# Two quarters of an up-projection weight moved from casting transfers on GpSimd's queue to plain transfers on SyncE's queue, with the cast done by three engines

## The chip, the core and the metric

The kernel runs on one core of one Trainium2 chip. A core has a matrix engine (TensorE; PE in the profile), three engines for elementwise work (VectorE, DVE; ScalarE, ACT; GpSimd, POOL), a queue engine (SyncE, SP) and 16 DMA engines that all queues share. Transfers can be issued by SP, ACT and POOL. In this kernel only those issued by POOL change the type on the way. The metric is the device time of one execution in microseconds (us): the kernel before took 323.79 us as the median of three runs (322.96 to 326.55).

## The reference

Sliding-window attention with a linear bias, followed by a two-layer feed-forward block with a hardswish between the layers. Eight batches, eight heads, 576 positions, head size 64, window 128; 4608 tokens, model size 512, inner size 2048. Everything is float32 outside the kernel.

```python
scores = (1/sqrt(64)) * q @ k.T            # per batch and head
scores = where((0 <= i-j) & (i-j < 128), scores + slope[h] * -(|i-j|), -1e9)
attn   = softmax(scores)
x      = (attn @ v)  -> [4608, 512]        # heads side by side
h      = x @ w_in                          # [512, 2048]
g      = h * clip(h + 3, 0, 6) / 6
out    = g @ w_out                         # [2048, 512]
```

## The kernel before

All matrix products are in bf16. The whole instruction order of each engine is written out by hand, so every engine works through its own list in that order and waits in place. A batch is four groups `g` of two heads; groups 0 to 3 are batch 0, groups 4 to 7 batch 1.

**Attention of one group.** k and q come as float32, are cast to bf16 (`prepare` for batch 0, `prepare_double` for batches 1 and 2), and are transposed on TensorE (`transposes`, `wide_double`, `double`) with a copy out of PSUM by DVE or ACT. `scores_diag` and `scores_off` compute the scores of the diagonal and of the preceding block, ACT takes the exponentials (`exp_diag`, `exp_off_full`), `attend` multiplies by v and DVE normalises. `back` transposes the result on TensorE into the one PSUM buffer `ps_o`, and ACT copies it into `xT`; for group 3 ACT copies 256 columns and DVE the rest. The next `back` cannot start before the last copy has emptied that buffer.

**Feed-forward.** Tokens are taken 512 at a time. `moe_up(nt, ms)` multiplies four slices `ks` of `w_in_sb`, 128 columns `ms` at a time, with the four group rows of `xT` (slice `ks` needs group `ks`), then ACT takes a ReLU (L470) and DVE the min and product into `gbuf[nt % 2]` (L471). `moe_down` multiplies by `w_out_sb` and DVE stores. `fill(n)` emits the next n such steps between the attention steps. `up_begin(nt, ms, n)` does the first n slices of a `moe_up` ahead.

**Weights.** `w_in_sb` is [128, 4, 2048] in bf16. It is loaded in four quarters of 512 columns by `load_w_in(g)` (L166): one transfer issued by POOL that reads 1 MB of float32 and writes 512 KB of bf16. Columns `ms` 0 to 3 are quarter 0, 4 to 7 quarter 1. Quarter 0 is issued by POOL among its casts of v of batch 0. Quarter 1 follows a one-column memset of `w_out_sb` (`second_w_in`, L176), which holds POOL until groups 0 and 1 have been attended. Quarters 2 and 3 come among the casts of k and q of batch 1.

**Loads.** SP issues, in this order: q of batch 0 (4 transfers; ACT issues the four of k), v of batch 0 (5, in 256-byte pieces), k and q of batch 1 (`load_double`, L98: k, k, q, q for the first two groups, then the same for the other two), v of batch 1 (5), k and q of batch 2. Each transfer issued by SP or ACT takes one of eight semaphores in turn, and so waits until the transfer eight places before it has landed.

**Buffers.** `gbuf[0]` and `gbuf[1]` are [128, 16, 512] bf16 each. `gbuf[0]` is first written by the L471 of `moe_up(0, 0)`, its upper half by `moe_up(0, 8)` and later. `gbuf[1]` holds the exponentials of batch 1 (its upper half those of groups 6 and 7), and `w_out_sb` those of batch 0.

The end of `first_batch` and the few steps after it carry the change. The engines' lists there, in words:

- ACT: eight exponential passes of batch 0; the four copies of `back`; the ReLU of `moe_up(0, 0)`; a copy of transposed k (L256); two more ReLUs; the exponentials of group 4, and so on.
- POOL: the casts of v; the issue of quarter 0; the memset and the issue of quarter 1; the casts of k, q of batch 1, groups 4 and 5 (four), then of groups 6 and 7 (k, k, issue of quarter 2, q, q, issue of quarter 3).
- TensorE: `attend` and `back` of groups 0 to 3, `up_begin(0, 0, 3)` ahead of `back(3)`, the transposes of q (`wide_double`), `up_begin(0, 1, 3)`, the rest of `moe_up(0, 0)`, the transposes of k, `moe_up(0, 1)` and `(0, 2)`, the transposes of k of groups 6 and 7, the scores of group 4.

Of the kernel before, what the change touches and what calls it, by code (L numbers as in the profile page):

```python
# [10 lines left out]
FP32 = mybir.dt.float32  # L11
# [7 lines left out]
def kernel(  # L19
# [9 lines left out]
    nc = tc.nc  # L29
# [13 lines left out]
    n_ms = d_ff // 128  # L43
    n_ks = d_model // 128
# [9 lines left out]
    w_in_sb = perm.tile([128, n_ks, d_ff], BF16)  # L54
    w_out_sb = perm.tile([128, n_ms, d_model], BF16)
# [22 lines left out]
    gbuf = [held.tile([128, n_ms, NT], BF16, name=f"gbuf{i}") for i in range(2)]  # L78
# [17 lines left out]
    def load_double(b, dp, nm, eng):  # L96
        for e in range(2):
            eng.dma_start(out=ldbuf["qk".index(nm)][:, ds((2 * dp + e) * RT * D, RT * D)],  # L98
                          in_=src_of[nm][b, ds(4 * dp, 4), :, :].rearrange(
                              "(i e) (a t) d -> e a i (t d)", e=2, t=RT)[e])  # L100
# [7 lines left out]
    def load_tokens(b, nm):  # L108
        t = tokens(b, nm)
        for j in range(NQ):  # L110
            n = min(128, S - j * 128)
            nc.sync.dma_start(out=t[:n, j, :, :],
                              in_=src_of[nm][b, :, ds(j * 128, n), :].rearrange("h p d -> p h d"))

    def constants():
        make_identity(nc, ident)
        nc.vector.memset(bias3, 0.5)
        nc.vector.memset(warm, 0.0)
        nc.scalar.activation(out=warm, in_=warm, func=ACT.Exp)
        nc.gpsimd.iota(rel_i, pattern=[[0, 1]], base=0, channel_multiplier=1)  # L120
        base = rpool.tile([128, NT], FP32, tag="r6", name="base")
        base_i = base[:, 0:256].bitcast(INT32).rearrange("p (s c) -> p s c", s=2)
        base_b = base[:, 256:384].bitcast(BF16).rearrange("p (s c) -> p s c", s=2)
        nc.gpsimd.iota(base_i, pattern=[[128, 2], [0, 128]], base=-192, channel_multiplier=1)
        nc.gpsimd.tensor_copy(out=base_b, in_=base_i)
        biases()
        nc.gpsimd.affine_select(out=base_b[:, 1, :], in_=base_b[:, 1, :], pattern=[[1, 128]],
                                channel_multiplier=-1, base=0,
                                compare_op=ALU.is_ge, fill=-(2.0 ** 30))
        nc.gpsimd.affine_select(out=base_b[:, 0, :], in_=base_b[:, 0, :], pattern=[[-1, 128]],  # L130
                                channel_multiplier=1, base=-1,
                                compare_op=ALU.is_ge, fill=-(2.0 ** 30))
        nc.vector.memset(kTb[0][:, :, 4, LAST:128], 0.0)
        for h in range(H):
            nc.vector.tensor_scalar(out=tab[:, h, :, :], in0=base_b, scalar1=slopes[h] / scale,
                                    scalar2=0.0, op0=ALU.mult, op1=ALU.add)
# [28 lines left out]
    def load_w_in(g):  # L165
        nc.gpsimd.dma_start(  # L166
            out=w_in_sb[:, :, ts(g, 512)],
            in_=moe_w_in[:, ts(g, 512)].rearrange("(k p) f -> p k f", p=128))

    def load_w_out(g):  # L170
        nc.gpsimd.dma_start(
            out=w_out_sb[:, ts(g, 4), :],
            in_=moe_w_out[ds(g * 512, 512), :].rearrange("(m p) d -> p m d", p=128))

    def second_w_in():
        nc.gpsimd.memset(w_out_sb[:, 4, 0:1], 0.0)  # L176
        load_w_in(1)

    def cast_v(b, j, copy):
        n = min(128, S - j * 128)  # L180
# [42 lines left out]
    def prepare_double(b, dp, copies, nms="kq", early=None):  # L223
        for nm, copy in zip(nms, copies):
            pr = prs.tile([128, RT, 2 * D], BF16, tag=f"pr{nm}", name="pr2")
            for e in range(2):
                copy(out=pr[:, :, ts(e, D)],  # L227
                     in_=ldbuf["qk".index(nm)][:, ds((2 * dp + e) * RT * D, RT * D)].rearrange(
                         "p (t d) -> p t d", t=RT))
                if early and (nm, e) == (nms[0], 0):  # L230
                    early()
            st[b, dp, nm] = pr
# [15 lines left out]
    def wide_double(b, dp, nm, copy):  # L248
        src = st[b, dp, nm]
        wide = ps_sc.tile([128, 2, 512], FP32, tag="sc", name="tp3")  # L250
        tp = wide.rearrange("p s c -> p (s c)").bitcast(BF16)[:, 0:RT * 128].rearrange(
            "p (t c) -> p t c", t=RT)
        for t in range(RT):
            nc.tensor.transpose(tp[:, t, :], src[:, t, :], ident)  # L254
        dst = (qTb if nm == "q" else kTb)[b % 2][:, 2 * dp:2 * dp + 2, :, :]
        copy(out=dst.rearrange("p i j c -> p i (j c)")[:, :, 0:S].rearrange(  # L256
                 "p i (a t) -> p i a t", t=RT),
             in_=tp.rearrange("p t (a i) -> p i a t", i=2))
# [147 lines left out]
    def attend(g):  # L406
        wide = ps_sc.tile([128, 2, 512], FP32, tag="sc", name="wide")
        av = wide[:, :, 0:NQ * W].rearrange("p e (j c) -> p e j c", j=NQ)
        av_matmuls(g, range(NQ), lambda qt, e: av[:, e, qt, :])
        avs = st[g, "avs"] = small.tile([128, NQ, 2, D], BF16, tag="avs", name="avs")  # L410
        rc = small.tile([128, 2, NQ, 1], FP32, tag="rcw", name="rcw")
        nc.vector.reciprocal(rc, av[:, :, :, D:W])
        nc.vector.tensor_tensor(out=avs.rearrange("p j e d -> p e j d"), in0=av[:, :, :, 0:D],
                                in1=rc.to_broadcast([128, 2, NQ, D]), op=ALU.mult)
# [40 lines left out]
    def up_begin(nt, ms, n):  # L455
        hps = ps_h.tile([128, NT], FP32, tag="h", name="hps")
        up_mms(nt, ms, 0, n, hps)
        begun[nt, ms] = hps, n
# [64 lines left out]
    def fill(n):  # L523
        for _ in range(n):
            if at[0] == len(units):
                return
            nt, fn, step = units[at[0]]
            if fn is moe_up and done[0] < NP * (min((nt * NT + NT - 1) // S, B - 1) + 1):
                return
            fn(nt if fn is moe_up else nt - 1, step)  # L530
            at[0] += 1
# [26 lines left out]
    def first_batch():  # L558
        prepare(0, (V, A))
        warm_up(20)  # L560
        tables_diag(0)
        tables_off(0)
        warm_up(10)
        transposes(0, (V, A))
        scores_diag(0)
        prepare(1, (P, V))
        transposes(1, (V, V))
        scores_off(0)
        exp_full(0)
        scores_diag(1)  # L570
        prepare(2, (P, P))
        tables_off(1)
        transposes(2, (V, V))
        scores_off(1)
        exp_full(1)
        scores_diag(2)
        prepare(3, (P, V))
        tables_off(2)
        transposes(3, (V, V))
        scores_off(2)  # L580
        exp_full(2)
        scores_diag(3)
        scores_off(3)
        exp_full(3)
        cast_v(0, 0, V)
        cast_v(0, 1, P)
        load_w_in(0)
        cast_v(0, 2, V)
        cast_v(0, 3, V)
        cast_v(0, 4, P)  # L590
        for dp in range(2):
            for nm in "kq":
                load_double(1, dp, nm, nc.sync)
        load_tokens(1, "v")
        attend(0)
        attend(1)
        back(0)
        attend(2)
        back(1)
        second_w_in()  # L600
        prepare_double(1, 0, (P, P))
        attend(3)
        back(2)
        up_begin(0, 0, 3)
        back(3)
        wide_double(1, 0, "q", V)
        prepare_double(1, 1, (P,), "k")
        load_w_in(2)
        prepare_double(1, 1, (P,), "q")
        load_w_in(3)  # L610
        for dp in range(2):
            for nm in "kq":
                load_double(2, dp, nm, nc.sync)
        up_begin(0, 1, 3)
        done[0] = NP
        fill(1)
        wide_double(1, 0, "k", A)
        fill(2)

    def second_batch():  # L620
# [97 lines left out]
    with tc.manual_schedule(engines=every):  # L718
        load_run(0, "k", nc.scalar)
        load_run(0, "q", nc.sync)  # L720
        load_run(1, "k", nc.scalar)
        load_run(1, "q", nc.sync)
        for g in (2, 3):
            load_run(g, "k", nc.scalar)
            load_run(g, "q", nc.sync)
        load_tokens(0, "v")
        constants()
        memsets()
        memsets_later()
        first_batch()  # L730
        second_batch()
        fill(2)
        segment(2 * NP, G, lambda g: FILLS.get(g, (1, 1, 1, 2, 0, 1, 2)))
        done[0] = G
        fill(len(units))
# [30 lines left out]
```

## Time and profile before

| | |
|---|---|
| median of three runs | 323.79 us (322.96 to 326.55) |
| the profiled execution's own time | 323.38 us |
| its span, first to last instruction | 321.7 us |
| TensorE busy | 308.1 us (96%) |
| ACT busy | 195.1 us (61%) |
| DVE busy | 172.7 us (54%) |
| POOL busy | 140.7 us (44%) |
| granted TensorE clock | 1.000 |
| the four transfers of w_in, issue to landing | median 9.2 us (6.5 to 10.4) |

Start times in the profile count from the first instruction of the span. The profiled execution's own time is 1.68 us above its span. A busy TensorE is not necessarily at its full rate, since the ends of its pipelined products are modelled. Lines are those of the kernel before; in the changed kernel the helpers from `cast_v` (L179) to `segment` have line numbers six or more higher, because of the lines added.

### The profile page before, as it was taken

What the parts mean: (1) busy time and instruction counts of PE and PEld (TensorE: products, weight loads), DVE (VectorE), ACT (ScalarE), POOL (GpSimd) and SP (SyncE); (2) the same over time, 40 slices, a digit from 0 to 9 for tenths busy, and PEclk for the clock granted to TensorE, in tenths of its full rate; (3) what the DMA queues carried; (4) which work ended last, traced back from release to release, by engine and by line L of the source; (5) the groups of instructions that cost most, each with busy time, mean ns of one, the idle gap of its engine ahead of it and who ended that gap; (6) DMA issues with size and microseconds to landing.
All of it is one profiled execution on the core that took longest, in us unless ns stands there. A gap on an engine that the chain in (4) does not pass through costs nothing.

```text
span 321.7 us, 7010 instructions
## 1 busy us (share of the span) xinstructions
PE 308.1 (96%) x2699; PEld 166.7 (52%) x2738; DVE 172.7 (54%) x338; ACT 195.1 (61%) x334; POOL 140.7 (44%) x249
## 2 busy tenths in 40 slices
PE   6879999999999999999999999999999999999996
PEld 5465465555555455455677644554554444444443
DVE  6657675554356555555555556555655455455510
ACT  4748976877777766666676657666764344244401
POOL 8456592683494767356745664563331000000000
PEclk9999999999999999999999999999999999999999
DMA  7999999899999999999999999932112200000112
GB/s 277 202 319 225 272 255 208 223 235 204 220 223 184 220 198 201 200 223 205 186 191 191 229 176 201 211 108 86 23 53 64 76 34 35 33 33 33 67 52 79
DMA packets 131425, 51.90 MB, mean 161 GB/s; under 512 B 118976, under 2 KB 123328, under 8 KB 131392
## 3 DMA queue, kind: packets, MB, share of 16 engines
q1 hardware_dynamic: 126160, 45.36, 67.0%
q0 software_dynamic: 4224, 4.19, 8.3%
q10 hardware_dynamic: 1008, 1.90, 1.6%
q8 instruction: 21, 0.34, 0.5%
q14 instruction: 12, 0.10, 0.1%
HBM read 36.70 MB, written 9.44 MB: 143 GB/s over the span
## 4 chain that ended last, share of the span: by engine, by line
PE 82%; DMA 5%; ACT 4%; POOL 4%; issue 2%; DVE 2%; SPq 1%; POOLq 0%
PE ops L501 35%; PE hps L451 35%; DMA ldbuf<-in_q_dram 3%; PE scd L296 2%; DMA qTb<-tbuf 2%; PE av L391 2%; PE av L383 2%; ACT r L470 2%; PE sco L328 1%; PE ops L482 1%; ACT kTb L244 1%; PE tp L254 1%; POOL tbuf L194 1%; ACT gbuf L351 1%; SPq L98 1%
## 5 line engine op out<-in xcount | busy, mean ns | idle before, releaser
L471 DVE SCALAR_TENSOR_TENSOR gbuf<-r,hps 128x512 bf16<-128x512 f32 x144 | 98.7, 687 | 102.5 <-ACT r L470 100.2
L470 ACT ACTIVATE r<-hps,bias 128x512 f32<-128x512 f32 x144 | 98.9, 689 | 89.5 <-PE hps L451 88.2
L451 PE MATMUL hps<-xT,w_in_sb 128*128 128x512 bf16 (+1 forms) x621 | 142.7, 358 | 2.3 <-DMA w_in_sb<-in_moe_w_in_dram 0.9
L501 PE MATMUL ops<-w_out_sb,gbuf 128*128 128x512 bf16 x540 | 134.2, 380 | 2.3 <-issue 1.7
L451 PEld LDWEIGHTS <-w_in_sb 128*128 128x128 bf16 x640 | 58.8, 98 | 54.8 <-DMA w_in_sb<-in_moe_w_in_dram 1.3
L501 PEld LDWEIGHTS <-gbuf 128*128 128x128 bf16 x560 | 52.2, 98 | 57.2
L354 POOL TENSOR_SCALAR_AFFINE_SELECT pd<-pd 128x512 bf16<-128x512 bf16 x48 | 29.6, 631 | 34.5 <-ACT pd L351 34.4
L364 POOL TENSOR_SCALAR_AFFINE_SELECT po<-po 128x512 bf16<-128x512 bf16 x48 | 30.1, 633 | 32.7 <-ACT po L361 32.6
L351 ACT ACTIVATE pd<-scd,bias_d 128x512 bf16<-128x512 f32 x48 | 31.6, 685 | 5.0 <-PE scd L296 3.6
L194 POOL CAST tbuf<-ldbuf 128x512 bf16<-128x512 f32 (+1 forms) x45 | 25.5, 611 | 18.7 <-DMA qTb<-tbuf 9.8
L510 DVE COPY osb<-ops 128x512 f32<-128x512 f32 x33 | 22.7, 687 | 20.3 <-PE ops L501 20.3
L361 ACT ACTIVATE po<-sco,bias_o 128x512 bf16<-128x512 f32 x48 | 33.1, 689 | 0.0
L402 DVE TENSOR_TENSOR avs<-av,rc 128x384 bf16<-128x384 f32 (+1 forms) x48 | 23.6, 491 | 1.6
L391 PEld LDWEIGHTS <-pd 128*128 128x128 bf16 x192 | 14.4, 97 | 8.3 <-issue 0.5
L383 PE MATMUL av<-vbuf,po 128*128 128x65 bf16 x192 | 18.1, 193 | 0.1
L391 PE MATMUL av<-vbuf,pd 128*128 128x65 bf16 x192 | 17.5, 194 | 0.3 <-ACT kTb L244 0.3
L383 PEld LDWEIGHTS <-po 128*128 128x128 bf16 x192 | 14.4, 98 | 3.1 <-DVE avs L402 0.5
L187 POOL CAST vbuf<-ldbuf 128x1024 bf16<-128x1024 f32 x14 | 14.3, 1040 | 3.2 <-DMA ldbuf<-in_v_dram 3.2
L367 ACT ACTIVATE p4buf<-sco,bias_d 128x64 bf16<-128x64 f32 x48 | 15.5, 324 | 0.0
L227 POOL CAST pr<-ldbuf 128x576 bf16<-128x576 f32 x20 | 12.8, 669 | 4.4 <-DMA ldbuf<-in_k_dram 3.4
L296 PE MATMUL scd<-qTb,kTb 64*128 64x128 bf16 x256 | 12.7, 219 | 1.8 <-DVE kTb L220 1.1
L296 PEld LDWEIGHTS <-kTb 64*128 64x128 bf16 x256 | 7.2, 94 | 13.5 <-issue 9.7
(96 smaller groups left out, 215.0 us busy)
## 6 DMA issues: line engine op xcount, KB each, us to landing
out_dram<-osb SPq DMA_DIRECT2D x33, 256.0 KB, 2.4
ldbuf<-in_v_dram SPq DMA_DIRECT2D x32, 256.0 KB, 5.3
ldbuf<-in_q_dram SPq DMA_DIRECT2D x20, 256.0 KB, 5.1
ldbuf<-in_k_dram SPq DMA_DIRECT2D x16, 256.0 KB, 4.6
ldbuf<-in_q_dram SPq DMA_DIRECT2D x12, 288.0 KB, 6.4
ldbuf<-in_k_dram SPq DMA_DIRECT2D x12, 288.0 KB, 6.4
w_in_sb<-in_moe_w_in_dram POOLq DMA_DIRECT2D x4, 512.0 KB, 9.2
w_out_sb<-in_moe_w_out_dram POOLq DMA_DIRECT2D x4, 512.0 KB, 11.1
```

Of the source, the lines that this page charges most:

```text
L194: nc.gpsimd.tensor_copy(out=tbuf[:m, :, j, :], in_=s[:m, j, :, :].rearrange("p (i e) d -> p i (e d)", e=2))
L296: nc.tensor.matmul(scd[:, e, ts(j, 128)], lhsT=kT[r, j, :], rhs=qT[r, j, :], start=first, stop=first or j == 3)
L351: nc.scalar.activation(out=pd[:, e, :, :].rearrange("p j c -> p (j c)"), in_=sc[:, e, :], func=ACT.Exp, bias=bias_d[:, h:h + 1], scale=scale)
L354: nc.gpsimd.affine_select(out=pd[:, e, :, :], in_=pd[:, e, :, :], pattern=[[0, 4], [1, 128]], channel_multiplier=-1, base=0, compare_op=AL ...
L361: nc.scalar.activation(out=po[:, e, :, :].rearrange("p j c -> p (j c)"), in_=sc[:, e, :], func=ACT.Exp, bias=bias_o[:, h:h + 1], scale=scale)
L364: nc.gpsimd.affine_select(out=po[:, e, :, :], in_=po[:, e, :, :], pattern=[[0, 4], [-1, 128]], channel_multiplier=1, base=-1, compare_op=A ...
L383: nc.tensor.matmul(out_av, lhsT=po[:, e, qt % 4, :], rhs=vb[:, qt - 1, h, :], start=True, stop=False)
L391: nc.tensor.matmul(out_av, lhsT=d, rhs=vb[:, qt, h, :], start=(qt == 0), stop=True)
L451: nc.tensor.matmul(hps[:, lo:hi], lhsT=w_in_sb[:, ks, ts(ms, 128)], rhs=xT[:, ks, ds(src, hi - lo)], start=(ks == 0), stop=(ks == n_ks - 1))
L470: nc.scalar.activation(out=r6, in_=hps, func=ACT.Relu, bias=bias3[:, 0:1], scale=1.0 / 6.0)
L471: nc.vector.scalar_tensor_tensor(out=gts[nt][:, ms, :], in0=r6, scalar=1.0, in1=hps, op0=ALU.min, op1=ALU.mult)
L501: nc.tensor.matmul(ops[nt, sub], lhsT=gts[nt][:, ms, ts(sub, 128)], rhs=w_out_sb[:, ms, :], start=(ms == 0), stop=(ms == n_ms - 1))
```

## The change

`load_raw(i)` loads quarter i of `w_in` as a plain float32 transfer of 1 MB, issued by SP, into the upper half of `gbuf[i]` seen as float32. `cast_raw(i, ks, copy)` casts one slice [128, 512] of it into `w_in_sb`. Quarter 0 is issued after v of batch 0 and ahead of k and q of batch 1, quarter 1 after the first half of k and q. Slices 0 and 1 of quarter 0 are cast by ACT, placed after the exponentials of group 3 and ahead of the copies of `back`; slices 2 and 3 by POOL, ahead of its casts of k and q of groups 4 and 5. Slices 0 and 1 of quarter 1 are cast by POOL ahead of the casts of groups 6 and 7, slice 2 by ACT behind its copy of transposed k, slice 3 by DVE. `up_begin(0, 0, 3)` becomes `up_begin(0, 0, 2)`. The POOL issues of quarters 0 and 1 and the memset are gone; quarters 2 and 3 stay as they were.

```diff
+    raw = [gb[:, n_ms // 2:n_ms, :].rearrange("p m c -> p (m c)").bitcast(FP32).rearrange(
+        "p (k f) -> p k f", k=n_ks) for gb in gbuf]
+
+    def load_raw(i):
+        nc.sync.dma_start(out=raw[i],
+                          in_=moe_w_in[:, ts(i, 512)].rearrange("(k p) f -> p k f", p=128))
+
+    def cast_raw(i, ks, copy):
+        copy(out=w_in_sb[:, ks, ts(i, 512)], in_=raw[i][:, ks, :])
-
-    def second_w_in():
-        nc.gpsimd.memset(w_out_sb[:, 4, 0:1], 0.0)
-        load_w_in(1)
...
         cast_v(0, 1, P)
-        load_w_in(0)
         cast_v(0, 2, V)
...
                 load_double(1, dp, nm, nc.sync)
+            if dp == 0:
+                load_raw(1)
         load_tokens(1, "v")
+        for ks in (0, 1):
+            cast_raw(0, ks, A)
         attend(0)
         attend(1)
         back(0)
         attend(2)
         back(1)
-        second_w_in()
+        for ks in (2, 3):
+            cast_raw(0, ks, P)
         prepare_double(1, 0, (P, P))
         attend(3)
         back(2)
-        up_begin(0, 0, 3)
+        up_begin(0, 0, 2)
         back(3)
         wide_double(1, 0, "q", V)
+        for ks in (0, 1):
+            cast_raw(1, ks, P)
         prepare_double(1, 1, (P,), "k")
...
         wide_double(1, 0, "k", A)
+        cast_raw(1, 2, A)
+        cast_raw(1, 3, V)
         fill(2)
...
         load_tokens(0, "v")
+        load_raw(0)
         constants()
```

## The prediction

> **What bounds the kernel now.** The page first: PE is busy 308.1 of 321.7 us, and the chain that ended last gives it 82%. From 52 us on TensorE hardly waits, so this change can act only before that. The chain of the first 50 us says through what:
>
> ```profile
> 14.50 8.26 DMA ldbuf<-in_q_dram
> 22.81 0.68 POOL pr L227
> 23.54 0.68 PE tp L254 x9
> 24.21 0.86 PE hps L451 x4
> ...
> 35.61 0.36 ACT r L470
> ...
> 42.14 0.72 ACT r L470
> 42.88 0.69 DVE gbuf L471
> ```
>
> It runs through the last q transfer of groups 4 and 5, its cast on POOL, TensorE, and from 35.6 through ACT. The timeline of ACT shows why:
>
> ```profile
> 16.61 1.02 ACT L335 ACTIVATE w_out_sb<-sco 128x1024 bf16<-128x1024 f32 x1
> 19.14 0.64 ACT L438 COPY xT<-tb 128x576 bf16<-128x576 bf16 x1 [1.51 <-PE tb L432]
> 20.30 0.64 ACT L438 COPY xT<-tb 128x576 bf16<-128x576 bf16 x1 [0.53 <-PE tb L432]
> 21.47 0.64 ACT L438 COPY xT<-tb 128x576 bf16<-128x576 bf16 x1 [0.53 <-PE tb L432]
> 23.28 0.37 ACT L434 COPY xT<-tb 128x256 bf16<-128x256 bf16 x1 [1.17 <-PE tb L432]
> 25.12 0.69 ACT L470 ACTIVATE r<-hps,bias 128x512 f32<-128x512 f32 x1 [1.46 <-PE hps L451]
> 25.70 1.11 ACT L256 COPY kTb<-tp 128x1152 bf16<-128x1152 bf16 x1
> 26.70 1.28 ACT L470 ACTIVATE r<-hps,bias 128x512 f32<-128x512 f32 x2
> ```
>
> From 25.10 to 42.85 the busy times by stretch give ACT 17.49 of 17.75 us: it has no room. TensorE shows 17.49 as well, partly modelled. So this stretch ends earlier only if ACT starts it earlier or does less in it. Before it there is room, 1.5 us in front of 19.14 for one. The timeline of TensorE has the only waits on w_in: 0.94 us for quarter 0 ahead of 22.37, and 0.4 us (in the waits) for quarter 1 near 28:
>
> ```profile
> 22.37 0.60 PE L451 MATMUL hps<-xT,w_in_sb 128*128 128x512 bf16 x2 [0.94 <-DMA w_in_sb<-in_moe_w_in_dram]
> ```
>
> Last the DMA queues, in 14 to 18 us (both queues busy) and 19 to 22 us (SP's queue q1 nearly alone):
>
> ```profile
> DMA packets 634, 0.76 MB, mean 190 GB/s; under 512 B 87, under 2 KB 491, under 8 KB 634
> q0 software_dynamic: 404, 0.41, 73.2%
> q1 hardware_dynamic: 230, 0.35, 32.4%
> ...
> DMA packets 595, 1.17 MB, mean 391 GB/s; under 512 B 68, under 2 KB 101, under 8 KB 595
> q1 hardware_dynamic: 556, 1.14, 98.6%
> ```
>
> q0 counts written bf16, so 0.41 MB stand for 0.82 MB read; with q1 that is 0.29 MB/us against 0.39 for plain transfers alone.
>
> **When raw quarter 0 lands.** SP finishes issuing v at 12.2 and issued k at 12.31; that transfer's packets begin near 14.5. So quarter 0 starts near 14.4. 1.05 MB at 391 GB/s is 2.7 us: last packet near 17.1. From last packet to landing v took 1.3 us (14.4 to 15.7), the first k transfers 2.2 (with quarter 0 beside them). So 18.4 to 19.3; I take 18.6, nearer the undisturbed row. Far ends: 17.8 (no tail beyond 0.7) and 20.6 (8.3 us, as q took from 14.4). SP's issue of it is not in the trace; loads in the same list cost 0.37 to 0.6 us when nothing blocks, and 2.0 for the last of v. k behind it would be issued 0.4 to 2 us later, under the cover of quarter 0's own 2.7 us of data. Beyond that each microsecond would move all below by one; I take 0.
>
> Behind it each k or q of 288 KB needs 0.75 us: the four for groups 4 and 5 land near 19.4, 20.2, 20.9, 21.7 (before: 18.6, 21.0, 21.8, 22.7). Raw quarter 1 follows at 24.0, the next k at 24.7 and 25.5 (24.2, 25.7), q at 26.2 and 27.0 (27.3, 28.4).
>
> By the Trainium skill (DMA: Bandwidth & Descriptors, Specifications) HBM gives a core about 358 GB/s; the trace has 391 over 3 us, which decides. By the page quarter 0 would land 0.25 us later, and so would the end.
>
> **What is added and removed, engine by engine.**
>
> *ACT, quarter 0.* Two casts of 128x512 behind the last exponential (done 17.6). The nearest row is ACT's 128x576 cast, 0.67 us; back to back ACT starts 0.58 apart. They wait for 18.6 and end at 19.8. Behind them in ACT's list is the first copy of `back`, which began at 19.14: 0.65 late. `back(1)` on TensorE waits for that copy (one buffer), so the cycle of 1.17 us per copy moves with it: third copy done at 22.8 (before 22.1). But `back(3)` ran only at 22.80, because `up_begin` ahead of it stood 0.94 us waiting for quarter 0. That wait goes, and `up_begin` has one product (0.22 us) less ahead of `back(3)`, which it gets back in `moe_up(0, 0)`. So `back(3)` runs at 22.8 as before: what the copies lose, the missing wait returns.
>
> *POOL, quarter 0.* Out: two issues (0.88, 0.74) and a memset. In: two casts; its own 128x512 cast took 0.62. From 18.6 to 19.85, then four casts at 0.67: 22.5, against 23.48 before.
>
> *TensorE.* `wide_double` of q began at 23.54, 0.47 behind the end of `back(3)`, waiting for POOL. Now it follows at 23.1. Nine transposes 0.5, five products 1.1: `moe_up(0, 0)` ends at 24.7, ACT's first ReLU starts at 24.75, 0.37 earlier.
>
> *ACT, quarter 1.* One more cast inside the full stretch: +0.58, nothing hides it. Its data (24.0) are there. So ACT runs +0.2 late from there.
>
> *POOL, quarter 1.* Two casts from 24.0 to 25.25, then k of groups 6 and 7 to 26.6. TensorE needs it for its transposes at 26.52 before; even or 0.1 late. ACT then has the ReLUs until 28.05, so this stays hidden up to 0.5 us. The issue of quarter 2 moves from 26.4 to 26.6; quarter 3 stays near 29. Both were far ahead of their use.
>
> *DVE, slice 3.* One cast, 0.42 by its own 128x512 row; it idled 0.91 us before 27.43. Nothing.
>
> *TensorE's 0.4 us wait for quarter 1* goes. It had made ACT idle: 17.75 less 17.49 is 0.26 us in the stretch. I credit 0.2.
>
> *v of batch 1* comes earlier (the last full one at about 32 instead of 37.9), so POOL's 2.94 us wait for it goes and POOL reaches w_out and the casts of batch 2 some 2 us earlier. None of the waits of 44 to 100 us on TensorE or ACT ends on a DMA, so nothing.
>
> Sum: -0.37 + 0.58 - 0.2 = 0.0 us. On the profiled execution's 323.38 us (span 321.7 and 1.68 around it) that is 323.4; against the median of 323.79, which lies 0.4 above it, **323.8**. One per cent is 3.2 us, about what this kernel's measurement can tell from no change, its three runs lying 1.1% apart.
>
> **Rivals.**
>
> *Quarter 0 lands late, and ACT waits: slower.* ACT's casts wait in front of the copies of `back`, and POOL's in front of k and q; before, a late quarter 0 held only TensorE at 22.1. From a landing at 18.5 every microsecond later is one at the end. For it: transfers in this window took 6.3 to 10.6 us to land, and 13 to 14 us shows v's tail spread unevenly over the engines. Against it: no second queue is left there. At 20.6 it costs 2.1 us (325.9). It passes 1% from a landing at 21.8, 9.5 us after issue; at 10.6 it is 4.3 us, 328.1. Past 1%: 0.17.
>
> *The FIFO rival: slower.* From 15 to 16.5 us q0 and q1 each had half the engines' time (56.5% both in the last 0.5 us); now k and q stand behind quarter 0 in one queue. If raw quarters run at the 190 GB/s of 14 to 18 us instead of 391, quarter 0 needs 5.5 us, lands at 21.2, and the last q of groups 4 and 5 near 24.3, cast by 25.0 against 23.48: 2.7 us for the first, not added to the 1.5 of the second, 326.5. The Trainium skill says so in DMA: Bandwidth & Descriptors, Queues, rings and completion order: engines take turns between queue rows packet by packet, within a row descriptors start in order. That agrees with the halves in the trace. I count its chance (0.10) as within 1%.
>
> *TensorE and not ACT is the bound: faster.* Then the casts on ACT are free and what counts are its waits: 0.94, 0.29 (for POOL's cast of q) and 0.4, together 1.6 us: 322.2. For it: the chain goes through TensorE from 23.5 to 34.8. Against: ACT's 17.49 of 17.75. Chance 0.10, within 1%. More, over 1%, would need POOL's earlier work at 40 us to count as well, up to 2 us more; 0.06.
>
> *It does not do what it says:* ACT's and POOL's quarter casts start only when the landing releases them, so if quarter 0 lands at 22 as now, it is the first rival.
>
> **Chances.** Forecast, within half a per cent: 0.57; the FIFO rival 0.10 and the TensorE rival 0.10, both within 1%: same 0.77. Slower by over 1% 0.17, faster 0.06. The range takes the far landings, 17.8 (-0.7, with the 0.7 of scatter under the median) and 20.6 (+2.1), and the FIFO rival's 326.5: 322.3 to 326.5.
>
> **What would show it.** Right: raw quarter 0 lands 6 to 7 us after issue; ACT's first cast starts between 18.3 and 19.3, `back`'s first copy near 19.8; no TensorE wait on w_in at 22; ACT's first ReLU near 24.75; DVE's L471 that followed 42.14 within 0.5 us of 42.9. Wrong: a landing past 20; a wait of TensorE for POOL's casts of groups 6 and 7 over 0.5 us; a shift of the end that does not exist at 43 us, which would mean that the later transfers count after all.

## The result, and the profile after

The changed kernel takes **324.69 us** (median; 324.13 to 325.64), the kernel before, run beside it, 323.58 (322.90 to 326.55). The ratio is **1.003, 95% interval 1.0018 to 1.0042**: some 1.0 us slower, inside the one per cent that counts as no change, but not nothing. The profiled execution took 324.85 us (span 323.1) against 323.38 (span 321.7), granted clock 1.000 in both.

The chain of the changed kernel's first 45 us, in order of time (start, us, what; pieces left out at "..."), runs through quite different work than before:

```profile
16.11 9.50 DMA gbuf<-in_moe_w_in_dram
...
25.66 0.76 POOL w_in_sb L178 x2
...
26.78 1.47 POOL pr L233 x2
28.25 0.15 POOL w_in_sb L166
...
29.08 1.22 POOL pr L233 x2
30.29 12.53 DMA w_in_sb<-in_moe_w_in_dram
...
42.87 0.39 PE hps L457
```

Where q of groups 4 and 5 led before, raw quarter 1 leads now: issued at 16.11, landed at 25.6. POOL casts two slices of it, then k of groups 6 and 7, and only then issues quarters 2 and 3, the last of which lands at 42.8. The timeline of TensorE has the two waits that follow (the bracket gives the idle time ahead of the instruction and what ended it):

```profile
28.30 0.68 PE L260 MATMUL tp<-ident,pr 128*128 128x128 bf16 x9 [1.28 <-POOL pr L233]
...
42.87 1.04 PE L457 MATMUL hps<-xT,w_in_sb 128*128 128x512 bf16 x3 [0.48 <-DMA w_in_sb<-in_moe_w_in_dram]
```

The waits for quarters 0 and 1 (0.94 and 0.4 us) are gone, as meant; in their place TensorE waits 1.28 us for POOL's cast of k of groups 6 and 7, whose transposes begin at 28.30 instead of 26.52. TensorE and ACT before, at the same two places:

```profile
26.52 0.68 PE L254 MATMUL tp<-ident,pr 128*128 128x128 bf16 x9
```

```profile
27.85 1.28 ACT L351 ACTIVATE gbuf<-scd,bias_d 128x512 bf16<-128x512 f32 x2
```

ACT after shows what the wait does:

```profile
17.34 1.02 ACT L341 ACTIVATE w_out_sb<-sco 128x1024 bf16<-128x1024 f32 x1
19.18 1.14 ACT L178 CAST w_in_sb<-gbuf 128x512 bf16<-128x512 f32 x2 [0.82 <-DMA gbuf<-in_moe_w_in_dram]
20.23 0.63 ACT L444 COPY xT<-tb 128x576 bf16<-128x576 bf16 x1
...
25.48 0.69 ACT L476 ACTIVATE r<-hps,bias 128x512 f32<-128x512 f32 x1 [1.39 <-PE hps L457]
26.07 1.11 ACT L262 COPY kTb<-tp 128x1152 bf16<-128x1152 bf16 x1
27.07 0.63 ACT L178 CAST w_in_sb<-gbuf 128x512 bf16<-128x512 f32 x1
27.59 1.28 ACT L476 ACTIVATE r<-hps,bias 128x512 f32<-128x512 f32 x2
29.35 1.27 ACT L357 ACTIVATE gbuf<-scd,bias_d 128x512 bf16<-128x512 f32 x2 [0.48 <-PE scd L302]
```

The first exponentials of group 4 begin at 29.35; before it was 27.85. These 1.5 us are still there at the end: 324.85 less 323.38 is 1.47. ACT stood idle for only 0.48 us of them. With k in time it would still have begun near 28.9, 1.0 us later than before: its first ReLU is 0.36 us later, and its cast of quarter 1 stands ahead. Two things are late here, and k is the later one.

POOL before, whose lines follow, cast the two k as they landed, at 24.4 and 25.8:

```profile
24.38 0.67 POOL L227 CAST pr<-ldbuf 128x576 bf16<-128x576 f32 x1 [0.90 <-DMA ldbuf<-in_k_dram]
25.80 0.67 POOL L227 CAST pr<-ldbuf 128x576 bf16<-128x576 f32 x1 [0.75 <-DMA ldbuf<-in_k_dram]
26.41 0.74 POOL L166 DMA_DIRECT2D w_in_sb<-in_moe_w_in_dram  x1
```

After:

```profile
25.66 1.18 POOL L178 CAST w_in_sb<-gbuf 128x512 bf16<-128x512 f32 x2 [2.03 <-DMA gbuf<-in_moe_w_in_dram]
26.78 1.47 POOL L233 CAST pr<-ldbuf 128x576 bf16<-128x576 f32 x2
28.20 0.89 POOL L166 DMA_DIRECT2D w_in_sb<-in_moe_w_in_dram  x1
```

Why raw quarter 1 landed at 25.6 and not at 24.0 shows in the DMA queues of the changed kernel, first in 14 to 15.5 us, then in 15.5 to 18, then in 18 to 25:

```profile
DMA packets 182, 0.19 MB, mean 124 GB/s; under 512 B 103, under 2 KB 103, under 8 KB 182
...
DMA packets 449, 0.91 MB, mean 363 GB/s; under 512 B 10, under 2 KB 10, under 8 KB 449
...
DMA packets 1341, 2.73 MB, mean 390 GB/s; under 512 B 104, under 2 KB 104, under 8 KB 1339
```

The rate of 390 GB/s held, from 18 us on. But the first 1.5 us, which still hold 103 packets under 512 B, as v's are, moved 0.19 MB where that rate would have moved 0.58: one microsecond behind from the start. The two raw quarters and the four k and q between them are 3.28 MB; 1.1 MB had gone by 18 us, the rest takes 5.6 us, so by this estimate the last packet goes near 23.6 and 2.0 us pass to the landing.

### The profile page after: what moved, and what is told of

Its sections match the earlier page's. It is cut to its first block, busy times and chain, and to the rows that moved or that the text cites. A ratio compares the mean times of both kernels' runs of the same rounds, so it can differ in the third digit from the quotient of the medians.

```text
span 323.1 us, 7020 instructions
## 1 busy us (share of the span) xinstructions
PE 308.9 (96%) x2699; PEld 167.8 (52%) x2738; DVE 173.8 (54%) x339; ACT 197.1 (61%) x337; POOL 141.4 (44%) x250
## 4 chain that ended last, share of the span: by engine, by line
PE 81%; DMA 9%; SPq 3%; ACT 2%; issue 2%; POOL 1%; DVE 1%; ACTq 0%
PE ops L507 36%; PE hps L457 35%; DMA w_in_sb<-in_moe_w_in_dram 4%; DMA gbuf<-in_moe_w_in_dram 3%; PE av L397 2%; PE scd L302 2%; SPq L112 2%; PE av L389 2%; DMA ldbuf<-in_k_dram 2%; PE sco L334 1%; DMA out_dram<-osb 1%; PE ops L488 1%; ACT kTb L250 1%; POOL pr L233 1%; SPq L98 1%
## 5 line engine op out<-in xcount | busy, mean ns | idle before, releaser
L457 PE MATMUL hps<-xT,w_in_sb 128*128 128x512 bf16 (+1 forms) x621 | 142.4, 357 | 1.9 <-DMA w_in_sb<-in_moe_w_in_dram 0.5
L457 PEld LDWEIGHTS <-w_in_sb 128*128 128x128 bf16 x640 | 59.0, 98 | 54.1 <-issue 0.8
L397 PEld LDWEIGHTS <-pd 128*128 128x128 bf16 x192 | 14.4, 97 | 8.3 <-issue 0.5
L397 PE MATMUL av<-vbuf,pd 128*128 128x65 bf16 x192 | 17.4, 194 | 0.3 <-ACT kTb L250 0.3
```

The costliest lines, as they stand in the source:

```text
L397: nc.tensor.matmul(out_av, lhsT=d, rhs=vb[:, qt, h, :], start=(qt == 0), stop=True)
L457: nc.tensor.matmul(hps[:, lo:hi], lhsT=w_in_sb[:, ks, ts(ms, 128)], rhs=xT[:, ks, ds(src, hi - lo)], start=(ks == 0), stop=(ks == n_ks - 1))
```

## The experiments

The theory to test, A: the loss is the lateness of k of groups 6 and 7, which stands behind raw quarter 1 in SP's queue and behind its two casts in POOL's list. The rivals: C, the late issue and landing of quarter 3 (the 0.48 us wait and the chain); D, the late landing of quarter 0, which holds ACT in front of the copies of `back`; and B, ACT's extra cast of 0.58 us. Letters in the expectations stand for these. Diffs are against the changed kernel. Each run is compared with the kernel before on the same chip.

**k ahead of quarter 1 on POOL (k_first).**

```diff
+        prepare_double(1, 1, (P,), "k")
         for ks in (0, 1):
             cast_raw(1, ks, P)
-        prepare_double(1, 1, (P,), "k")
```

> The changed kernel, but POOL casts k of groups 6 and 7 ahead of slices 0 and 1 of raw quarter 1. Theory A: the changed kernel lost its 1.1 us where TensorE waited 1.28 us for POOL's casts of that k, which stood behind raw quarter 1 (landed 25.6) and its two casts. Then the casts follow the landing of k itself (16.8 plus 9.6 is 26.4, the second near 27.0), end near 27.7 instead of 28.25, and the end comes 0.5 us earlier: 324.2 against 324.7. Theory B: the loss is the additional cast of 0.6 us on ACT, which is full from 25 to 44 us. Then nothing changes: 324.7.

Measured: 325.17 us, ratio 1.0052 (1.0034 to 1.0070), above what either theory gives. POOL in this kernel:

```profile
26.38 1.47 POOL L233 CAST pr<-ldbuf 128x576 bf16<-128x576 f32 x2 [2.83 <-DMA ldbuf<-in_k_dram]
27.80 1.17 POOL L178 CAST w_in_sb<-gbuf 128x512 bf16<-128x512 f32 x2
28.91 0.88 POOL L166 DMA_DIRECT2D w_in_sb<-in_moe_w_in_dram  x1
```

and TensorE:

```profile
27.91 0.68 PE L260 MATMUL tp<-ident,pr 128*128 128x128 bf16 x9 [0.96 <-POOL pr L233]
36.80 0.81 PE L457 MATMUL hps<-xT,w_in_sb 128*128 128x512 bf16 x3 [0.88 <-DMA w_in_sb<-in_moe_w_in_dram]
```

With nothing ahead of it, POOL stood 2.83 us for k and still finished its casts 1.4 us later than before. So of the 1.8 us by which the transposes were late, some 1.4 are the landing of k and 0.4 the casts in front of it. (Some 0.2 of the 1.4 is POOL's pair of casts itself, 1.47 us for the 1.29 that it takes in raw1_last below; DVE's cast of slice 3 runs beside it here.) The exponentials came 0.4 us earlier than in the changed kernel, 28.95; but the issue of quarter 2 moved back from 28.20 to 28.91, and TensorE paid 0.88 us for it at 36.80.

**Raw quarter 1 behind all k and q (raw1_last), and the same with ACT's cast given to DVE (last_act_free).**

```diff
-            if dp == 0:
-                load_raw(1)
+        load_raw(1)
         load_tokens(1, "v")
...
+        prepare_double(1, 1, (P,), "k")
         for ks in (0, 1):
             cast_raw(1, ks, P)
-        prepare_double(1, 1, (P,), "k")
```

> As k_first, and raw quarter 1 is issued behind k and q of groups 6 and 7 instead of ahead of them. Theory A: 1.05 MB less ahead of them, k lands 2.7 us earlier (near 24.3), TensorE's transposes of it start near 26.5 as in the kernel before, and the next limit is ACT, which is 0.9 us later there than before because of its cast and the 0.37 us later first ReLU: about 0.6 us gained, 324.1. Theory B: nothing, 324.7.

> raw1_last and act_free together. Theory A: with k early, ACT is the next limit, and so the cast now counts: 0.6 us beyond raw1_last, 323.5, even with the kernel before (323.6). Theory B: as act_free alone, 324.1.

Measured: 331.21 us (1.0224, 1.0190 to 1.0258) and 331.43 (1.0228, 1.0194 to 1.0262). Both expectations failed, and not through k, which came in time: POOL had cast it by 24.9. POOL in the first of the two:

```profile
23.60 1.29 POOL L233 CAST pr<-ldbuf 128x576 bf16<-128x576 f32 x2 [0.18 <-DMA ldbuf<-in_k_dram]
28.55 1.42 POOL L178 CAST w_in_sb<-gbuf 128x512 bf16<-128x512 f32 x2 [3.66 <-DMA gbuf<-in_moe_w_in_dram]
29.92 0.88 POOL L166 DMA_DIRECT2D w_in_sb<-in_moe_w_in_dram  x1
```

and TensorE:

```profile
41.46 1.49 PE L457 MATMUL hps<-xT,w_in_sb 128*128 128x512 bf16 x3 [4.62 <-DMA w_in_sb<-in_moe_w_in_dram]
```

POOL waited 3.66 us in place for quarter 1 with the issue of quarter 2 behind it. That quarter landed 11.1 us after its issue, TensorE stood 4.62 us, and the granted clock was 0.50 from 40.5 to 47.3 us. These are two costs that the changed kernel does not have; they say what a wait in front of POOL's issues can cost, not what the change costs. One thing these runs show all the same: in last_act_free, with k early and ACT's cast gone, the exponentials of group 4 begin at 27.77, 0.08 before those of the kernel before (quarter 0 landed early there, at 18.3). Nothing of the 1.5 us is left at that point; the stops that follow come from quarter 1 and quarter 2.

**ACT's cast of quarter 1 given to DVE (act_free).**

```diff
-        cast_raw(1, 2, A)
+        cast_raw(1, 2, V)
         cast_raw(1, 3, V)
```

> The changed kernel with slice 2 of raw quarter 1 cast by DVE instead of ACT, all else the same. Theory A: ACT stood waiting 0.48 us for TensorE behind that place anyway, so nothing is gained: 324.7, within 0.2. Theory B: ACT gets back 0.6 us: 324.1.

Measured: 324.67 us (1.0038, 1.0022 to 1.0054), as the changed kernel. ACT does 0.6 us less and gains nothing, for it now stands where the cast was, waiting for the scores of group 4:

```profile
29.93 1.26 ACT L357 ACTIVATE gbuf<-scd,bias_d 128x512 bf16<-128x512 f32 x2 [1.46 <-PE scd L302]
```

The exponentials are 0.6 us later still than in the changed kernel, and that is the landing of k again. SP issued this k at 17.27 here and at 16.80 there; it took 9.9 us to land, at 27.2, and POOL, done with quarter 1 at 26.7, began to cast it at 27.31. (The profile puts these 0.56 us of POOL down to TensorE's L457. But in the changed kernel POOL began the same cast at 26.78, while the same products of TensorE ran until 27.02, so it does not wait for them.) What this run shows is that the cast costs ACT nothing as long as k is later; it does not show that the cast is free with k in time.

**One quarter alone (q0_only, q1_only).** The other quarter stays POOL's casting transfer, as before.

```diff
 q0_only:
-            if dp == 0:
-                load_raw(1)
...
+        nc.gpsimd.memset(w_out_sb[:, 4, 0:1], 0.0)
+        load_w_in(1)
         for ks in (2, 3):
             cast_raw(0, ks, P)
...
-        cast_raw(1, 2, A)
-        cast_raw(1, 3, V)
 q1_only:
+        load_w_in(0)
...
-        for ks in (0, 1):
-            cast_raw(0, ks, A)
...
-        load_raw(0)
```

> Only quarter 0 goes by the plain transfer, quarter 1 by POOL's casting transfer as before (memset and issue), placed behind POOL's two casts of quarter 0. Theory A (the loss sits where raw quarter 1 and its casts stand ahead of k of groups 6 and 7): no wait of TensorE for that k beyond 0.3 us; quarter 1 is issued near 20.4 instead of 17.97 and lands between 28.4 and 30.8, of which up to 2 us are waited for: 323.2 to 325.5, and the loss, if any, shows as a wait for w_in. Theory D (the loss is quarter 0's late landing, which holds ACT's first copy of back 1.09 us longer): the whole loss stays, 324.7, with no wait for w_in needed to explain it.

> Only quarter 1 goes by the plain transfer, quarter 0 by POOL's casting transfer as before. Theory A: TensorE waits for k of groups 6 and 7 by 1 us or more and the loss stays: 324.4 to 325.2. Theory D: the copies of back stand as before and the loss goes: 323.5.

Measured: quarter 0 alone 323.73 us (1.0021, 1.0006 to 1.0037), quarter 1 alone 324.39 (1.0041, 1.0026 to 1.0057). With quarter 0 alone the exponentials of group 4 begin at 27.90, where they were before, and no wait for k is seen; the profiled execution, 323.34 us, equals that of before (323.38). With quarter 1 alone TensorE waits for k as in the changed kernel:

```profile
27.73 0.68 PE L260 MATMUL tp<-ident,pr 128*128 128x128 bf16 x9 [1.41 <-POOL pr L233]
```

So quarter 1 by itself makes a loss as large as that of both. Quarter 0 alone adds about 0.6 us to the median, by its interval's middle, which no line of its profile shows; the two do not add up. In the profiled execution of q0_only quarter 0 had landed by 18.5:

```profile
18.52 1.14 ACT L178 CAST w_in_sb<-gbuf 128x512 bf16<-128x512 f32 x2
```

In other kernels that issue it in the same place it lands as late as 19.9. Whether the executions behind the median are such is not known, since only one is profiled.

**Quarter 3 issued directly behind quarter 2 (w3_early).**

```diff
         load_w_in(2)
-        prepare_double(1, 1, (P,), "q")
         load_w_in(3)
+        prepare_double(1, 1, (P,), "q")
```

> The changed kernel with POOL's issue of quarter 3 directly behind that of quarter 2, ahead of its two casts of q: about 1.3 us earlier. Theory C (the end is set by quarter 3, issued 1.2 us later than before and landed at 42.8, for which TensorE waits 0.5 us): that wait goes, 0.5 us gained, 324.2. Theory A alone: ACT is as late as before at 43 us, nothing gained, 324.7.

Measured: 324.37 us (1.0041, 1.0026 to 1.0056). The wait at 42.87 is gone, TensorE waits 1.40 us for k, and the exponentials begin at 29.01. The median lies between the two forecasts, and by the ratio, 1.0041 against 1.003, nothing was gained. The chain led through quarter 3 in the changed kernel, but it is not what was paid for.

**k of groups 6 and 7 cast by DVE (k_dve, then k_dve2).** In the first, the cast was written behind the loads of batch 2, so DVE waits for these and groups 6 and 7 are scored with the k of batch 2; the time tells nothing of the theory. The second has it in its place.

```diff
-        prepare_double(1, 1, (P,), "k")
+        prepare_double(1, 1, (V,), "k")
         load_w_in(2)
```

> The changed kernel with k of groups 6 and 7 cast by DVE (0.45 us each, behind its L477 of moe_up(0, 0)) instead of POOL. POOL then issues quarter 2 at 26.9 and quarter 3 near 29.7, and TensorE gets k near 27.6 instead of 28.25. Theory A and C: both the wait for k (0.6 us shorter) and the one for quarter 3 shrink: 324.0. Theory D: nothing, 324.7.

> The changed kernel, with DVE instead of POOL casting k of groups 6 and 7, at its place in the order as written. Theory (half of the loss is POOL's two casts of raw quarter 1 in front of k, half the later landing of k): casts from 26.4 to 27.4 us, transposes at 27.5 (28.3 in the changed kernel, 26.5 before), exponentials of group 4 near 28.7, quarter 2 issued by 27.5: 324.0 us (1.002 of before). Rival (the landing alone, 27.0 for the second k, or DVE and POOL slow each other): transposes at 28 or later, 324.7 us (1.004).

Measured: the first 341.98 us (1.0583, 1.0561 to 1.0605), TensorE standing 17.4 us and the clock at 0.50 from 30.5 to 47.6. The second 324.34 (1.0031, 1.0015 to 1.0047). Its DVE and TensorE:

```profile
25.71 1.47 DVE L233 CAST pr<-ldbuf 128x576 bf16<-128x576 f32 x2 [0.35 <-DMA ldbuf<-in_k_dram]
```

```profile
27.25 0.68 PE L260 MATMUL tp<-ident,pr 128*128 128x128 bf16 x9 [0.75 <-DVE pr L233]
```

The transposes come 1.05 us earlier than in the changed kernel and the exponentials at 28.46, 0.9 earlier. But the larger part of that is this execution's: POOL had raw quarter 1 at 25.00 here, and at 25.66 in the changed kernel's profile:

```profile
25.00 1.17 POOL L178 CAST w_in_sb<-gbuf 128x512 bf16<-128x512 f32 x2 [2.04 <-DMA gbuf<-in_moe_w_in_dram]
```

That leaves some 0.4 us for DVE, what k_first gave for the casts in front of k. The profiled execution, 323.58 us, lies 0.76 below its kernel's median, and the ratio is that of the changed kernel (1.003): a gain in time is not shown. And ACT now goes from its ReLUs to the exponentials without a wait:

```profile
27.05 1.51 ACT L476 ACTIVATE r<-hps,bias 128x512 f32<-128x512 f32 x2
28.46 1.26 ACT L357 ACTIVATE gbuf<-scd,bias_d 128x512 bf16<-128x512 f32 x2
```

With k this much earlier ACT is the limit, 0.6 us behind the kernel before, and so its cast of quarter 1 counts. Theory A holds for the first part of the loss only.

**Quarter 0's casts between the copies of `back`, quarter 1 as before (q0_between).** The version meant to beat both.

```diff
-        for ks in (0, 1):
-            cast_raw(0, ks, A)
         attend(0)
         attend(1)
         back(0)
+        cast_raw(0, 0, A)
         attend(2)
         back(1)
+        cast_raw(0, 1, A)
+        nc.gpsimd.memset(w_out_sb[:, 4, 0:1], 0.0)
+        load_w_in(1)
         for ks in (2, 3):
             cast_raw(0, ks, P)
```

(and quarter 1's plain load and casts left out as in q0_only)

> Only quarter 0 is plain, as in the run that had quarter 0 alone (323.73 us, 1.002 of before), but ACT's two casts of it stand behind the first and the second copy of back, and POOL issues quarter 1 ahead of its own two casts. Theory (the casts cost only where they stand in front of back's copies and of the issue of quarter 1): first copy back at 19.1 us, copies at 19.1, 20.3 and 21.5, the wait of TensorE for w_in near 28 goes, first product of moe_down at 51.5 to 51.9, about 322.9 us (0.998 of before). Rival (ACT's list from 25 us has constant length and begins with k and q, which quarter 0 delays in SP's queue): exponentials of group 4 at 27.9 as before, 323.7 us (1.002).

Measured: 323.49 us, ratio 1.0000 (0.9983 to 1.0016). The copies ran at 19.14, 20.33 and 21.49, as wanted, and the wait for w_in went. But quarter 0 landed at 19.8 here, POOL's four casts of k and q began 1.1 us behind that, and TensorE waited for them instead:

```profile
23.56 0.68 PE L260 MATMUL tp<-ident,pr 128*128 128x128 bf16 x9 [0.94 <-POOL pr L233]
```

The 0.94 us that quarter 0 had cost in front of `up_begin` before stand here again, one step later. No version was found that is faster than the kernel before.

**raw1_last with the issues of quarters 2 and 3 ahead of quarter 1's casts (raw1_last_w_first).**

```diff
 (as raw1_last, and:)
         prepare_double(1, 1, (P,), "k")
-        for ks in (0, 1):
-            cast_raw(1, ks, P)
         load_w_in(2)
         prepare_double(1, 1, (P,), "q")
         load_w_in(3)
+        for ks in (0, 1):
+            cast_raw(1, ks, P)
```

> As the run in which raw quarter 1 is issued behind all k and q (331.2 us), but POOL casts k, issues quarter 2, casts q and issues quarter 3 before it turns to the two slices of raw quarter 1. Theory (the 6 us more of that run came from the issues of quarters 2 and 3 held behind the landing of raw quarter 1): quarter 2 issued near 27, no wait of TensorE over 1 us at 41 us, granted clock 1.0 in 40 to 48 us; what is left is the wait of ACT and TensorE for raw quarter 1, which lands near 28.5, 1 to 2 us: 324.2 to 325.2 us. Rival (the late raw quarter itself costs them): 330 us or more.

Measured: 325.40 us (1.0069, 1.0042 to 1.0096), 0.2 above the expected range. Quarter 2 was issued at 25.02, no wait at 41 us, clock 1.00 in 40 to 48: six of the eight microseconds were the held issues and the clock behind them, as the theory said. What is left is ACT, 0.61 us for quarter 1 at 29.05, and an earlier stop, TensorE's on the first copy of `back`, because quarter 0 landed at 19.9 in the profiled execution:

```profile
21.63 0.69 PE L438 MATMUL tb<-ident,avs 128*128 128x128 bf16 x5 [2.21 <-ACT xT L444]
```

The stretch by windows (PE, PEld, DVE, ACT, POOL busy, granted clock, DMA share, GB/s) shows the clock after it:

```profile
22.00:23.00 1.00, 1.00 (x20) 1.00 (x18) 0.00 (x0) 0.64 (x1) 0.94 (x3) 0.50 1.09 388
```

**Quarter 0 behind k and q of groups 4 and 5 (raw0_late).**

```diff
             if dp == 0:
+                load_raw(0)
                 load_raw(1)
...
-        load_raw(0)
```

> The changed kernel, with raw quarter 0 issued behind k and q of groups 4 and 5, directly ahead of raw quarter 1, so that it lands near 22 us and not at 19.2; k and q of groups 4 and 5 land earlier for it. Prediction's rival (a late quarter 0 holds ACT in front of the copies of back, 1 us at the end for each us): first copy of back at 23, first ReLU near 28, 327 us (1.011 of before). Theory that only the k of groups 6 and 7 sets the end: their place in the queue is the same, so 324.7 us (1.004).

Measured: 329.32 us (1.0174, 1.0149 to 1.0199). Quarter 0 landed at 23.0. ACT, then TensorE:

```profile
23.05 1.14 ACT L178 CAST w_in_sb<-gbuf 128x512 bf16<-128x512 f32 x2 [4.52 <-DMA gbuf<-in_moe_w_in_dram]
```

```profile
24.78 0.69 PE L438 MATMUL tb<-ident,avs 128*128 128x128 bf16 x5 [4.22 <-ACT xT L444]
```

Quarter 0 landed 3.9 us later than in the changed kernel, and the end came 4.6 us later: the prediction's rival, at more than its price of one for one, since the clock stood at 0.50 from 24.0 to 30.8 us. D is a real mechanism; at the changed kernel's landing of 19.2 the lateness of k covered it.

**All in one table.** From the profiled executions: the start of TensorE's transposes of k of groups 6 and 7, of the first exponentials of group 4, the execution's own time, and the difference of the last two.

| kernel | transposes | exponentials | own time | difference |
|---|---|---|---|---|
| before | 26.52 | 27.85 | 323.38 | 295.53 |
| q0_only | 26.55 | 27.90 | 323.34 | 295.44 |
| q0_between | 26.73 | 28.09 | 323.12 | 295.03 |
| k_dve2 | 27.25 | 28.46 | 323.58 | 295.12 |
| q1_only | 27.73 | 28.78 | 324.03 | 295.25 |
| k_first | 27.91 | 28.95 | 325.46 | 296.51 |
| w3_early | 27.96 | 29.01 | 324.35 | 295.34 |
| **after** | 28.30 | 29.35 | 324.85 | 295.50 |
| act_free | 28.88 | 29.93 | 325.19 | 295.26 |
| raw1_last_w_first | 28.13 | 30.73 | 325.84 | 295.11 |
| raw0_late | 32.64 | 34.51 | 329.46 | 294.95 |

These are single executions. In kernels that issue the raw quarters alike, quarter 0 landed anywhere from 18.3 to 19.9 and quarter 1 from 25.0 to 25.7, so half a microsecond between two rows need not be the edit's. Within an execution, though, the rows agree: over 6.7 us of shift the difference stays at 295.3 within 0.4. Only k_first, which waits 0.88 us for quarter 2 at 36.80, lies above. In these kernels what happens behind the exponentials of group 4 takes a constant time; what starts them decides. In before, q0_only, q0_between and k_dve2 ACT comes to them straight from its ReLUs, so it is ACT's own list. From q1_only to act_free it is the cast of k of groups 6 and 7; in raw1_last_w_first it is ACT, whose list is late by quarter 0 and by its wait for quarter 1, and in raw0_late the late copies of `back` with the half clock behind them. Not in the table are raw1_last, last_act_free and k_dve, which stop TensorE for 4.6 us and more.

## Why the prediction was right, and where not

The time held: 323.8 forecast against 324.69, within one per cent. The sum of 0.0 was wrong by the 1.1 us between the medians, 1.5 in the profiled executions. That the number held owes something to luck: the first ReLU came 0.73 us later than forecast, ACT's cast stood in its list as feared and k was 1.8 us late, but they did not add up, since only the last of them starts the exponentials of group 4. The range of 322.3 to 326.5 had room for any of them.

- **Landing of raw quarter 0** (18.6, between 18.4 and 19.3): right, 19.18 by ACT's first cast, 6.7 us after issue; from 18.3 to 19.9 in the other kernels that issue it in the same place.
- **The step that failed: raw quarter 1 at 24.0, and "even or 0.1 late, hidden up to 0.5" for POOL's k of groups 6 and 7.** The quarter landed at 25.6 and k was cast by 28.25 instead of 26.6. Two sizes were off. The full rate of 391 GB/s was taken from 14.4 us on, while the queue reached it only after 15.5; and the tail from last packet to landing was 2.0 us, not 1.3. My own terms, 21.7 and 2.7, made 24.4, not the 24.0 that I wrote. The mechanism, k behind POOL's casts of quarter 1, was named; its size was 1.8 us, past the 0.5 that the ReLUs hide. That is 1.3 over the cover, against a loss of 1.1 by the medians and 1.5 in the profiles.
- **ACT's cast of quarter 1, "+0.58, nothing hides it":** in the changed kernel the wait for k hides it (act_free). But it hides it by 0.48 us only, and where k comes earlier (k_dve2) ACT is the limit and the cast counts. The reading of ACT as the next limit was right; the wait in front of it was missing.
- **DVE's slice 3, "Nothing":** wrong by some 0.2 us. POOL's pair of k ran beside it and took 1.47 us, 1.29 in raw1_last without it.
- **First ReLU 0.37 earlier:** it came 0.36 later, 25.48, and so `back(3)` at 23.24. The copies start 1.1 us late and not 0.65, because quarter 0 landed at 19.2 and not at 18.6. In this execution it did not show at the end, since k was later still: TensorE reached its wait for k with 1.28 us in hand.
- **The waits of TensorE for w_in go:** right for quarters 0 and 1. The credit of 0.2 us was not seen at the end, for the wait for k stands in its place.
- **Quarters 2 and 3 "far ahead of use":** wrong for quarter 3, which landed at 42.8, 12.5 us after issue, and stopped TensorE for 0.48 us. Without that wait (w3_early) no gain could be told. Quarter 2 is the near one: 0.7 us more delay cost 0.88 us (k_first).
- **v of batch 1 earlier:** wrong, POOL cast its last full v at 37.89 (37.95 before). It was credited nothing.
- **The rivals.** The late quarter 0 exists, at 1.2 us per us (raw0_late), but at the landing of 19.2 the wait for k covered it. The FIFO rival's half rate did not come: 390 GB/s. Its other half did: within SP's queue k waits behind the raw quarter. By the Trainium skill (DMA: Bandwidth & Descriptors, Queues, rings and completion order) each DMA engine takes the descriptors of a row in order; the trace agrees, k landing 0.7 us behind the quarter in k_dve2 (25.66 and 25.0). TensorE as the bound, 322.2 us, did not come, for a longer wait took the place of the three that it counted; its other half, that the casts on ACT are free, held behind that wait (act_free).

The signs that the prediction had set for itself spoke against it: a wait of TensorE for POOL's casts of groups 6 and 7 over 0.5 us (1.28), and the L471 expected within 0.5 us of 42.9 came at 44.73. Open are the 0.6 us that quarter 0 alone adds to the median with nothing late in its profile, and a version that removes the lateness of k and shows it in the median: k_first and k_dve2 did the first by 0.4 us and not the second. That k is what sets the end rests on the traces, and on the medians of the single quarters.

## What to carry to other kernels

A transfer put into a queue is paid for by what stands behind it in that queue, and a cast put into an engine's list by what stands behind it there, the engine's own DMA issues included: follow both lists to the next use, not only the transfer that becomes faster. Charge a queue its ramp and its tail, each about a microsecond or two here, and not the full rate from the first packet. And before crediting the end of a wait, ask which wait comes next on the same engine: here one of 0.94 us was exchanged for one of 1.28, and right behind that one stood ACT's list, 0.48 us from being the limit itself.

## What the runs showed of the hardware

**The clock after a stop.** TensorE's granted clock fell to 0.50 in stops of 4.2 (raw0_late), 4.6 and 4.7 (raw1_last, last_act_free) and 17.4 us (k_dve). It fell once in a stop of 2.21 us (raw1_last_w_first), 2.0 us after the stop began, but not in stops of 1.88 and 2.12 us (raw1_last, last_act_free at 30.50). It stayed at 0.50 for 6.8 us in each of the first three, for 17.1 in k_dve and for 3.4 in raw1_last_w_first: each time a multiple of 3.4. The Trainium skill (TensorE: Matmul & The Clock Gate, Part 1: The HAM clock gate) has the clock halve after an idle window of 3.4 us; here 2.2 us sufficed once. So a wait just over two microseconds can cost more than itself: the five products of `back` behind it took 0.69 us, 0.45 in the changed kernel.

**DVE beside POOL.** DVE's 128x512 cast of slice 3 met POOL's pair of k in the changed kernel and in w3_early. In the changed kernel POOL had begun first (26.78), and DVE took 0.92 us:

```profile
26.81 0.92 DVE L178 CAST w_in_sb<-gbuf 128x512 bf16<-128x512 f32 x1
```

In w3_early DVE began first, POOL at 26.40, and DVE took 0.42:

```profile
26.35 0.42 DVE L178 CAST w_in_sb<-gbuf 128x512 bf16<-128x512 f32 x1
```

POOL's pair took 1.47 and 1.50 us there, 1.29 in raw1_last, where DVE cast nothing beside it. The Trainium skill (SBUF — State Buffer, Who interferes with whom) says that a DVE instruction in a two-port mode, which a cast can enter, and a GpSimd instruction contend for one port pair: the first to issue holds it for the whole instruction, and the other waits. The trace agrees, with 0.42 us for DVE's cast where it began first and 0.92 where it began second.

**The landing of a casting transfer.** Quarter 3, issued by POOL at 29.09 before and at 30.29 after, landed at 37.7 and 42.8: 8.6 and 12.5 us for the same bytes. Quarters 2 and 3 of raw1_last took 11.1 and 14.4. What makes the difference, SP's loads beside them for one, was not tried.
